# Weight passes three steps later, early high stores, first MoE products after the products with v, and MoE operands at multiples of 512 bytes

## The chip, the cores and the metric

The kernel runs on one core of a Trainium2 chip. The number that counts is the device time of one execution in microseconds (us). Before the change the median of three runs is 692.88 us (692.36 to 696.8).

## What is computed

An attention layer with a learned position bias, and behind it an MLP with a rational activation. Shapes: 4 batches, 8 heads, 576 positions, head width 64; then 2304 tokens of width 512 and a hidden width of 2048.

```python
scores = scale * np.matmul(q, k.transpose(0, 1, 3, 2)) + bias   # bias: 8 heads x 576 x 576, from a small MLP
attn = np.exp(scores - scores.max(-1))                          # divided by its sum + 1e-9
x = (attn @ v).transpose(0, 2, 1, 3).reshape(2304, 512)
h = x @ w_in
P = a[0] + a[1] * h + a[2] * h**2 + a[3] * h**3
Q = 1.0 + abs(b[0]) * abs(h) + abs(b[1]) * h**2
out = (P / (Q + 1e-6)) @ w_out
```

All inputs are float32, except that `w_in` and `w_out` arrive as float64.

## The kernel before

**Attention** is 72 steps, `step_a(i)`. In a step TensorE (PE) makes the scores of one block of queries for a pair of heads (`sc`, L324, float32), transposes the weights `p` of two steps ago (`tp` and a small piece in `mx`, L393), and multiplies the transposed weights `pt` of three steps ago with `v` (into `mx`, L433). VectorE (DVE) adds the bias and takes the row maximum `m` (L334); ScalarE (ACT) makes the exponential (L350) and a copy of `tp` (L401); DVE copies the rest of it and the result `xs` (L412, L443). GpSimd (POOL) multiplies `xs` with the reciprocal sums (`e_norm`, L382), one per pair of heads and batch; these go through DRAM (`xd`) and come back as the MoE input `xr`.

**Weight passes.** The MoE multiplies in a reduced float32 kind, with every operand split into a high and a low part. While the attention runs, the float64 weights are turned into such pairs, piece by piece: 16 pieces (`f`) for each of the two matrices. A piece is loaded as `wx` and `wy` (SP queue, L120, L121) and goes through `mag` (DVE, L130, makes `wk`), `rebias` (ACT, L135, makes `wh`), `sign` and `join` (DVE, L138, L144), `low` (POOL, or DVE for the last six of `f`, L156, makes `wil`, `wol` or `wl`) and `store` (SP queue, L160 into `wih` or `woh`, or to DRAM as `ws`, L107 and L108). `wk` has one buffer; `wh`, `wl`, `wx` and `wy` have two, so that the third piece's `rebias` waits for the first one's store to land. `in_order` lays all these out in one list, and `run_jobs`, at the end of every attention step, works it off up to and with one DVE pass.

**MoE** is 48 steps over 12 groups of 384 tokens, with the weights in four groups: groups 0 to 2 stand in tiles `wih0` to `wol2`, the fourth is cut out of a bias tile that has become free (`wg`). Each step has 24 matmuls `h <- x * w_in` (`mm1`, L300, 384 columns; the moving operand is `xh` or `xl`, the stationary one `wih` or `wil`) and, for the step two before, 18 matmuls `o <- g * w_out` (L766, 512 columns; moving `woh` or `wol`, stationary `gh` or `gl`). Between the two stands the activation on ACT, POOL and DVE: `w`, `u`, `t`, `r`, then `gh` (DVE, L714), `m` (L721, L728) and `gl` (POOL, L735). The tokens of an even group are held in tiles of pool `xp`, those of an odd group in `xp2`. The remaining weight passes (the late six) run beside the first 25 or so MoE steps on DVE.

Where a tile begins in a partition of SBUF is set by the order and size of the tiles allocated before it, from the left end for some pools and from the right end for others. In the built program the offsets in a partition, taken modulo 512 bytes, are 448 for `wih`, `wil`, `woh`, `wol` of groups 0 to 2 and for `xh`, `xl` of even groups; they are 64 for `wg`, for `xh`, `xl` of odd groups, and for `gh`, `gl`.

Of the kernel before, what the change touches and what calls it, by code (L numbers as in the profile page):

```python
# [16 lines left out]
P = 128  # L17
# [16 lines left out]
def tile_attn_moe(  # L34
# [49 lines left out]

    stg = ctx.enter_context(tc.tile_pool(name="stg", bufs=2))
# [19 lines left out]
    def w_out_to(f, part, hi, lo):  # L105
        d = dpool.tile([P, 2, KD, P], F32, tag=f"ws{f}_{part}", name=f"ws{f}_{part}")
        nc.sync.dma_start(out=d[:, 0], in_=hi.bitcast(F32))  # L107
        nc.sync.dma_start(out=d[:, 1], in_=lo.bitcast(F32))  # L108
        wsc[f, part] = d

    def w_conv(f, part):
# [21 lines left out]

        def rebias():
            A.activation(out=tl("wh", U32, 2), in_=st["wk"], func=AF.Relu, bias=wmin, scale=8.0)  # L135

        def sign():
            V.scalar_tensor_tensor(  # L138
                out=st["wh"], in0=st["u"], scalar=0x80000000, in1=st["wh"],
                op0=ALU.bitwise_and, op1=ALU.bitwise_or,  # L140
            )

        def join():
            V.scalar_tensor_tensor(  # L144
                out=tl("wk", U32), in0=st["m"], scalar=13, in1=st["wh"],
                op0=ALU.logical_shift_right, op1=ALU.bitwise_or,
            )

        def low():
            x, hi = st["wk"].bitcast(F32), st["wh"].bitcast(F32)  # L150
            if here:
                out = w_hilo(f, part)[1]
                x, hi = (v.rearrange("p (k f) -> p k f", k=KD) for v in (x, hi))
            else:
                out = tl("wl", F32R, 2)
            eng.tensor_tensor(out=out, in0=x, in1=hi, op=ALU.subtract)  # L156

        def store():
            if here:
                nc.sync.dma_start(  # L160
                    out=w_hilo(f, part)[0].bitcast(F32),
                    in_=st["wh"].bitcast(F32).rearrange("p (k f) -> p k f", k=KD),
                )
                return
            w_out_to(
                f, part, st["wh"].rearrange("p (k f) -> p k f", k=KD),
                st["wl"].rearrange("p (k f) -> p k f", k=KD),
            )
# [3 lines left out]
    def w_plain(f, part):  # L172
        st = {}

        def load():
            st["x"] = stg.tile([P, KD, P], F32, tag="wx", name=f"wx{f}_{part}")
            nc.sync.dma_start(out=st["x"], in_=w_src(f, part))

        def hi():
            st["h"] = stg.tile([P, KD, P], F32R, tag="wh", name=f"wh{f}_{part}")  # L180
            A.copy(out=st["h"], in_=st["x"])

        def lo():
            st["l"] = stg.tile([P, KD, P], F32R, tag="wl", name=f"wl{f}_{part}")
            V.tensor_tensor(out=st["l"], in0=st["x"], in1=st["h"].bitcast(F32), op=ALU.subtract)

        return [load, [], [hi], [lo, lambda: None, lambda: w_out_to(f, part, st["h"], st["l"])]]
# [4 lines left out]
    def in_order(jobs, after):  # L192
        seq = [("sp", j[0]) for j in jobs[:2]]
        end = []
        for i, (_, first, act, last) in enumerate(jobs):
# [3 lines left out]
            seq += [("dve", x) for x in ops[1:]] + [("low", low)]  # L199
            if i + 2 < len(jobs):  # L200
                seq.append(("sp", jobs[i + 2][0]))
            end = [("sp", x) for x in [store] + after.get(i, [])]
# [15 lines left out]
    with tc.manual_schedule():  # L218
# [3 lines left out]
        with ExitStack() as actx:  # L222
# [266 lines left out]
            def step_a(i):  # L489
# [25 lines left out]
                if i == NS + 1:  # L515
                    mm1(0, 1)
                if ok(TL + 1):
                    pv = e_pv(i - TL - 1, mx)
                if ok(0):
# [7 lines left out]
                if i == NS - 1:  # L527
                    mm1(0, 0)
# [22 lines left out]
                if i >= 2:  # L551
                    run_jobs(i >= 5 and (c > 0 or g % 2 == 0))
# [116 lines left out]
            G.memset(wpool.tile([P, 8], F32, tag="edge", name="edge"), 0.0)  # L669
# [266 lines left out]
```

## Time and profile before

| | us |
|---|---|
| median of three runs | 692.88 |
| the profiled execution | 693.02 |
| its span (first to last instruction) | 691.2 |
| PE busy | 671.3 (97%) |
| DVE busy | 578.1 (84%) |
| ACT busy | 484.8 (70%) |
| POOL busy | 233.8 (34%) |

The profiled execution lies 1.8 us outside its span, and 0.1 us above the median. Matmuls overlap, so a busy PE is not a PE at its peak: how fast it runs is read from the distance between the starts of like matmuls. The page also follows the chain of work that ended last back from the end and gives each engine's share of it. In a timeline row, the bracket at the end says how long the engine stood idle before the row and whose end released it.

### The profile page before, as it was taken

Reading aid. Unit: us, or ns where it says so; the run is one execution under the profiler, and the core shown is the slowest. Engines: PE = TensorE matmul, PEld = TensorE weight load, DVE = VectorE, ACT = ScalarE, POOL = GpSimd, SP = SyncE. Lnnn points to the kernel's source line nnn. Section 1 sums busy time; section 2 is a strip of 40 time slices with the busy share of each in tenths; the row PEclk is TensorE's granted clock in tenths of the full one; section 3 lists DMA queues with packets and bytes.
Section 4 is the critical chain, followed back from the end, with each engine's and each line's share of the span. In section 5 each row is a group of like instructions: output and inputs, shape, how many; then the busy total and the mean of one; then the engine's idle time right before and its main releaser. Section 6 shows DMA issues by size and latency. Waiting matters only on the chain.

```text
span 691.2 us, 16655 instructions
## 1 busy us (share of the span) xinstructions
PE 671.3 (97%) x6450; PEld 577.8 (84%) x6450; DVE 578.1 (84%) x1032; ACT 484.8 (70%) x758; POOL 233.8 (34%) x144
## 2 busy tenths in 40 slices
PE   6999899999999999999999999999999999999997
PEld 3777688888878778888999999999999999999995
DVE  7995788888878787499999999999968787878666
ACT  5888688889898888576666757676755565655561
POOL 0010032212312221164444544444444445344442
PEclk9999999999999999999999999999999999999999
DMA  4887998988898997324444443579621212122021
GB/s 139 310 310 222 352 306 267 319 260 272 295 342 278 299 334 252 98 105 157 160 169 143 134 177 135 169 226 297 231 91 47 92 46 92 46 91 93 1 92 46
DMA packets 77583, 129.50 MB, mean 187 GB/s; under 512 B 12208, under 2 KB 33856, under 8 KB 77504
## 3 DMA queue, kind: packets, MB, share of 16 engines
q1 hardware_dynamic: 76640, 126.77, 54.7%
q10 hardware_dynamic: 864, 1.67, 0.8%
q8 instruction: 51, 0.84, 0.5%
q14 instruction: 28, 0.23, 0.1%
HBM read 89.65 MB, written 35.61 MB: 181 GB/s over the span
## 4 chain that ended last, share of the span: by engine, by line
PE 85%; DVE 5%; DMA 4%; issue 2%; ACT 2%; SPq 1%; POOL 0%; DVEq 0%; ACTq 0%; POOLq 0%
PE o L766 27%; PE h L300 27%; PE mx L433 11%; PE sc L324 10%; PE tp L393 5%; PE pb L635 5%; DMA wih<-wh 2%; DVE ring L597 1%; DVE gh L714 1%; DMA ws<-wh 1%; PE mx L393 1%; DMA wy<-in_w_in_dram 1%; ACT pt L401 1%; DMA cst<-in_cst_dram 1%; DMA tab<-e 1%
## 5 line engine op out<-in xcount | busy, mean ns | idle before, releaser
L696 POOL TENSOR_TENSOR u<-u,w 128x768 f32<-128x768 f32 x48 | 96.7, 2015 | 159.1 <-ACT u L694 155.5
L334 DVE CUSTOM_DVE_ANT_0 s<-sc,bias 128x576 f32<-128x576 f32 x144 | 103.6, 754 | 18.7 <-PE sc L324 11.5
L350 ACT ACTIVATE p<-s,m 128x576 f32<-128x576 f32 x144 | 110.7, 772 | 1.5 <-DVE m L334 1.1
L693 ACT ACTIVATE w<-h 128x768 f32<-128x768 f32 x48 | 39.0, 813 | 102.1 <-PE h L300 102.1
L735 POOL TENSOR_TENSOR gl<-m,r 128x768 fp32r<-128x768 f32 x47 | 87.2, 1855 | 57.0 <-DVE m L728 54.9
L300 PE MATMUL h<-xl,wih 128*128 128x384 f32 x288 | 97.0, 337 | 0.3 <-DVE xl L286 0.3
L300 PE MATMUL h<-xh,wih 128*128 128x384 f32 x288 | 97.3, 338 | 0.0
L300 PE MATMUL h<-xh,wil 128*128 128x384 f32 x288 | 97.0, 337 | 0.0
L324 PE MATMUL sc<-k,q 64*128 64x288 f32 (+1 forms) x640 | 92.6, 428 | 4.0 <-DVE m L334 4.0
L433 PE MATMUL mx<-pt,v 128*64 128x128 f32 (+1 forms) x1600 | 95.6, 268 | 0.9 <-DVE xs L443 0.9
L401 ACT COPY pt<-tp 128x1024 f32<-128x1024 f32 x72 | 72.3, 1005 | 20.5 <-PE tp L393 20.3
L766 PE MATMUL o<-woh,gh 128*128 128x512 f32 x216 | 85.2, 395 | 0.0
L766 PE MATMUL o<-wol,gh 128*128 128x512 f32 x216 | 85.1, 394 | 0.0
L433 PEld LDWEIGHTS mx<-pt,v 128*64 128x64 f32 x1600 | 79.1, 137 | 6.1 <-ACT u L694 1.1
L700 ACT ACTIVATE r<-u,qc 128x768 f32<-128x768 f32 x48 | 45.1, 940 | 36.8 <-POOL u L696 36.3
L324 PEld LDWEIGHTS sc<-k,q 64*128 64x128 f32 (+1 forms) x640 | 50.3, 175 | 24.4 <-DVE m L334 9.1
L704 DVE TENSOR_TENSOR t<-t,h 128x768 f32<-128x768 f32 x48 | 45.5, 949 | 30.0 <-ACT t L695 24.5
L721 DVE SCALAR_TENSOR_TENSOR m<-u,qc,gh 128x768 f32<-128x768 f32 x48 | 61.8, 1288 | 5.4 <-DVE gh L714 0.5
L728 DVE SCALAR_TENSOR_TENSOR m<-t,cst,m 128x768 f32<-128x768 f32 x48 | 64.2, 1337 | 1.7
L714 DVE SCALAR_TENSOR_TENSOR gh<-t,cst,r 128x768 fp32r<-128x768 f32 x48 | 56.5, 1176 | 8.2 <-ACT r L701 5.8
L766 PE MATMUL o<-woh,gl 128*128 128x512 f32 x216 | 56.2, 395 | 0.0
L300 PEld LDWEIGHTS h<-xl,wih 128*128 128x128 f32 x288 | 54.1, 188 | 2.1 <-DVE xl L286 0.7
(73 smaller groups left out, 1284.3 us busy)
## 6 DMA issues: line engine op xcount, KB each, us to landing
tab<-e SPq DMA_DIRECT2D x36, 295.5 KB, 4.3
wx<-in_w_in_dram SPq DMA_DIRECT2D x16, 512.0 KB, 5.5
wy<-in_w_in_dram SPq DMA_DIRECT2D x16, 512.0 KB, 6.3
wx<-in_w_out_dram SPq DMA_DIRECT2D x16, 512.0 KB, 4.5
wy<-in_w_out_dram SPq DMA_DIRECT2D x16, 512.0 KB, 5.9
xr<-xd SPq DMA_DIRECT2D x7, 768.0 KB, 6.8
ws<-wh SPq DMA_DIRECT2D x20, 256.0 KB, 2.0
ws<-wl SPq DMA_DIRECT2D x20, 256.0 KB, 2.9
```

Of the source, the lines that this page charges most:

```text
L300: T.matmul(hps[s][:, j, :TT], w[:, k, sl], x[:, k, :], start=(k == 0 and z == 0), stop=(k == KD - 1 and z == 2),)
L324: T.matmul(sc[i, j][o, a, :SH], q[r, x], k[r, a * SH:(a + 1) * SH], start=True, stop=True,)
L334: V.tensor_tensor_reduce(out=t.rearrange("p (a s) -> p a s", a=2), in0=sc.pop((i, j))[:, :, :SH], in1=bias[p][:, 5 * j + c, :].rearrange(" ...
L350: A.activation(out=prob[i][:, z * S:z * S + S], in_=t, func=AF.Exp, bias=m, scale=-1.0, accum_out=sums[u % 4][:, k:k + 1],)
L401: A.copy(out=t[:, 0:8].rearrange("p x (r s) -> p r x s", r=2), in_=ps)
L433: T.matmul(ps[y, o], vt[n][:, kc, y], t[:, 2 * kc + j if kc < 4 else 8, o], start=(kc == 0), stop=(kc == 4),)
L696: G.tensor_tensor(out=u, in0=u, in1=w, op=ALU.mult)
L714: V.scalar_tensor_tensor(out=hi, in0=rt[s, "t"], scalar=abs_[:, 0:1], in1=rt[s, "r0"], op0=ALU.add, op1=ALU.mult,)
L721: V.scalar_tensor_tensor(out=m, in0=rt[s, "u"], scalar=qc, in1=rt[s, "gh"].bitcast(F32), op0=ALU.add, op1=ALU.mult,)
L728: V.scalar_tensor_tensor(out=m, in0=rt[s, "t"], scalar=abs_[:, 0:1], in1=m, op0=ALU.add, op1=ALU.subtract)
L735: eng.tensor_tensor(out=lo, in0=rt[s, "m"], in1=rt[s, "r0"], op=ALU.mult)
L766: T.matmul(po[n, c], l[:, j, c * P:(c + 1) * P], r[fp][:, j, :], start=(first and x is a), stop=(last and x is z),)
```

## The change

Four things change; no operation of DVE or ACT gets another shape.

1. **Where tiles begin.** A tile of 448 bytes per partition (`fill`, with one small memset on POOL) is put ahead of the pools on the left, and the tile `edge` on the right grows from 32 to 480 bytes. In the built program `wih`, `wil`, `woh`, `wol`, `wg`, `xh`, `xl`, `gh`, `gl` and the activation's tiles now all begin at offset 0 modulo 512. Of the attention's tiles, `p` goes from 448 to 384 while the constant `ident` stays at 128; `q` and `k`, and `pt` and `v`, move together.
2. **The store in two.** The high part's store is issued right after `join`, ahead of `low` and of the next piece's loads; the low part's store (to DRAM only) stays where the whole store was.
3. **When passes run.** The DVE passes begin at step 8 instead of 5, loads at step 4 instead of 2, and no step is left out any more (before, steps 11, 29, 47 and 65 had none). So a pass stands three steps later until step 11, two until 29, one until 47, at its old step until 65, and one step earlier behind that.
4. **The first MoE products.** `mm1(0, 0)` moves from the end of step 71 to step 72 behind its products with `v`, and `mm1(0, 1)` in step 73 from before them to behind them.

```diff
+    fill = cpool.tile([P, 112], F32, tag="fill", name="fill")
+    nc.gpsimd.memset(fill[:, 0:8], 0.0)
...
-            seq += [("dve", x) for x in ops[1:]] + [("low", low)]
+            seq += [("dve", x) for x in ops[1:]] + [("sp", lambda st=store: st(True, False)), ("low", low)]
             if i + 2 < len(jobs):
                 seq.append(("sp", jobs[i + 2][0]))
-            end = [("sp", x) for x in [store] + after.get(i, [])]
+            end = [("sp", x) for x in [lambda st=store: st(False, True)] + after.get(i, [])]
...
-                if i == NS + 1:
-                    mm1(0, 1)
                 if ok(TL + 1):
                     pv = e_pv(i - TL - 1, mx)
+                if 0 <= i - NS < 2:
+                    mm1(0, i - NS)
...
-                if i == NS - 1:
-                    mm1(0, 0)
...
-                if i >= 2:
-                    run_jobs(i >= 5 and (c > 0 or g % 2 == 0))
+                if i >= 4:
+                    run_jobs(i >= 8)
...
-            G.memset(wpool.tile([P, 8], F32, tag="edge", name="edge"), 0.0)
+            G.memset(wpool.tile([P, 120], F32, tag="edge", name="edge"), 0.0)
```

`store(hi, lo)` issues for a piece that stays in SBUF the one copy of the high part, and for the others the high or the low part's copy to DRAM.

On PE at the change from attention to MoE, before (`h0` and `h1` are the products `mm1` of the first two MoE steps, one row standing for twelve or more; `mx72` to `mx74` and `tp70`, `tp71` belong to steps 72 to 74):

```order
L300 MATMUL h0_5168<-xh0_4512,wih0_934 128x384
...
L393 MATMUL mx72_5189<-ident_60,p70_5114 128x64 x2
L393 MATMUL tp70_5191<-ident_60,p70_5114 128x64 x16
L433 MATMUL mx72_5189<-pt69_5129,v15_4586 64x128 x10
L393 MATMUL mx73_5225<-ident_60,p71_5166 128x64 x2
L393 MATMUL tp71_5227<-ident_60,p71_5166 128x64 x16
...
L300 MATMUL h0_5168<-xl0_4513,wih0_934 128x384
L300 MATMUL h0_5168<-xh0_4512,wil0_935 128x384
L433 MATMUL mx73_5225<-pt70_5190,v15_4586 64x128 x10
L433 MATMUL mx74_5279<-pt71_5226,v15_4586 64x128 x10
L300 MATMUL h1_5298<-xh0_4512,wih1_938 128x384
```

The same place after:

```order
L391 MATMUL mx72_5178<-ident_60,p70_5116 128x64 x2
L391 MATMUL tp70_5180<-ident_60,p70_5116 128x64 x16
L431 MATMUL mx72_5178<-pt69_5131,v15_4590 64x128 x10
L298 MATMUL h0_5210<-xh0_4514,wih0_936 128x384
...
L391 MATMUL mx73_5227<-ident_60,p71_5168 128x64 x2
L391 MATMUL tp71_5229<-ident_60,p71_5168 128x64 x16
...
L431 MATMUL mx73_5227<-pt70_5179,v15_4590 64x128 x10
L298 MATMUL h0_5210<-xl0_4515,wih0_936 128x384
L298 MATMUL h0_5210<-xh0_4514,wil0_937 128x384
L431 MATMUL mx74_5281<-pt71_5228,v15_4590 64x128 x10
L298 MATMUL h1_5300<-xh0_4514,wih1_940 128x384
```

Twelve `h0` matmuls now stand between the products of `pt69` and the transposes of `p71`, and the other twelve between the products of `pt70` and those of `pt71`, which were back to back.

On the SP queue near the start of the weight passes, before (`q2` to `v2` are operands of the third pair of heads):

```order
L120 DMA wx0_0_990<-in_w_in_dram 128x1024
L121 DMA wy0_0_991<-in_w_in_dram 128x2048
L120 DMA wx0_1_994<-in_w_out_dram 128x1024
L121 DMA wy0_1_995<-in_w_out_dram 128x2048
L253 DMA q2_1048<-in_qt_dram 128x576
L254 DMA k2_1049<-in_kt_dram 128x576
L260 DMA v2_1152<-in_vp_dram 128x640
```

After:

```order
L251 DMA q2_1042<-in_qt_dram 128x576
L252 DMA k2_1043<-in_kt_dram 128x576
L123 DMA wx0_0_1095<-in_w_in_dram 128x1024
L124 DMA wy0_0_1096<-in_w_in_dram 128x2048
L123 DMA wx0_1_1099<-in_w_out_dram 128x1024
L124 DMA wy0_1_1100<-in_w_out_dram 128x2048
L258 DMA v2_1152<-in_vp_dram 128x640
```

The four loads of the first two pieces are now behind `q2` and `k2`; their first use on DVE is three steps later. Further on, a high store stands ahead of the next loads on this queue, where it stood behind them.

## Rows read from the trace of the kernel before

**Rows 1.** The page: each engine's share of the chain that ended last.
```profile
PE 85%; DVE 5%; DMA 4%; issue 2%; ACT 2%; SPq 1%; POOL 0%; DVEq 0%; ACTq 0%; POOLq 0%
```
**Rows 2.** Windows: stretch, us, busy PE, PEld, DVE, ACT, POOL, PEclk, DMA share, GB/s.
```profile
60.00:80.00 20.00, 17.06 (x240) 13.49 (x238) 11.38 (x36) 13.06 (x27) 0.71 (x1) 0.91 0.88 306
240.00:260.00 20.00, 18.80 (x308) 15.70 (x308) 17.09 (x53) 17.47 (x36) 4.14 (x3) 1.00 0.97 319
```
**Rows 3.** Timeline of PE, scores of steps 5 to 8: start, us, instruction, idle before.
```profile
63.73 1.24 PE L324 MATMUL sc<-k,q 64*128 64x288 f32 x8
66.70 1.20 PE L324 MATMUL sc<-k,q 64*64 64x288 f32 x16
72.79 2.09 PE L324 MATMUL sc<-k,q 64*128 64x288 f32 x7 [2.94 <-DVE m L334]
77.99 1.24 PE L324 MATMUL sc<-k,q 64*128 64x288 f32 x8
```
**Rows 4.** Timeline of the SP queue and of DVE: the first piece's load and pass.
```profile
66.85 0.43 SPq L120 DMA_DIRECT2D wx<-in_w_in_dram  x1
71.63 0.43 DVE L130 TENSOR_SCALAR wk<-wx 128x512 uint32<-128x512 uint32 x1 [4.32 <-DMA wx<-in_w_in_dram]
```
**Rows 5.** Timeline of ACT: two passes that waited for a store.
```profile
190.78 0.72 ACT L135 ACTIVATE wh<-wk,wmin 128x512 uint32<-128x512 uint32 x1 [2.39 <-DMA wih<-wh]
231.68 0.72 ACT L135 ACTIVATE wh<-wk,wmin 128x512 uint32<-128x512 uint32 x1 [2.31 <-DMA ws<-wh]
```
**Rows 6.** Timeline of PE: the scores around those two passes.
```profile
189.97 1.24 PE L324 MATMUL sc<-k,q 64*128 64x288 f32 x8
194.33 1.24 PE L324 MATMUL sc<-k,q 64*128 64x288 f32 x8
230.88 1.20 PE L324 MATMUL sc<-k,q 64*64 64x288 f32 x16
235.23 1.24 PE L324 MATMUL sc<-k,q 64*128 64x288 f32 x8
```
**Rows 7.** Timeline of PE where the MoE begins.
```profile
281.03 0.28 PE L393 MATMUL mx<-ident,p 64*128 64x64 f32 x2 [0.68 <-DVE xs L443]
286.27 1.31 PE L433 MATMUL mx<-pt,v 128*64 128x128 f32 x20 [0.87 <-DVE xs L443]
```
**Rows 8.** Timeline of PE: first and last of four stretches of like matmuls.
```profile
411.01 0.33 PE L300 MATMUL h<-xh,wih 128*128 128x384 f32 x1
...
414.48 0.34 PE L300 MATMUL h<-xh,wil 128*128 128x384 f32 x1
...
414.65 0.39 PE L766 MATMUL o<-woh,gh 128*128 128x512 f32 x1
...
417.20 0.40 PE L766 MATMUL o<-wol,gh 128*128 128x512 f32 x1
...
424.40 0.39 PE L766 MATMUL o<-wg,gh 128*128 128x512 f32 x1
...
426.89 0.40 PE L766 MATMUL o<-wg,gl 128*128 128x512 f32 x1
...
444.08 0.34 PE L300 MATMUL h<-xl,wih 128*128 128x384 f32 x1
...
447.95 0.34 PE L300 MATMUL h<-xh,wil 128*128 128x384 f32 x1
```
**Rows 9.** Windows, columns as in rows 2: four MoE steps with weight passes.
```profile
326.70:360.20 33.50, 33.50 (x170) 30.36 (x169) 32.67 (x34) 21.54 (x29) 15.72 (x8) 1.00 0.46 153
```
**Rows 10.** Timeline of POOL: `gl` of MoE steps 3 and 23.
```profile
321.04 1.84 POOL L735 TENSOR_TENSOR gl<-m,r 128x768 fp32r<-128x768 f32 x1 [3.17 <-DVE m L728]
...
485.92 1.87 POOL L735 TENSOR_TENSOR gl<-m,r 128x768 fp32r<-128x768 f32 x1
```
**Rows 11.** Timeline of DVE: the same operation twice.
```profile
300.01 2.61 DVE L714 SCALAR_TENSOR_TENSOR gh<-t,cst,r 128x768 fp32r<-128x768 f32 x1
...
497.71 1.00 DVE L714 SCALAR_TENSOR_TENSOR gh<-t,cst,r 128x768 fp32r<-128x768 f32 x1
```

More of the change, by code (lines that the diff above doesn't have):

```diff
@@ L105, in w_out_to @@
     def w_out_to(f, part, hi, lo):
-        d = dpool.tile([P, 2, KD, P], F32, tag=f"ws{f}_{part}", name=f"ws{f}_{part}")
-        nc.sync.dma_start(out=d[:, 0], in_=hi.bitcast(F32))
-        nc.sync.dma_start(out=d[:, 1], in_=lo.bitcast(F32))
+        d = wsc.get((f, part)) or dpool.tile([P, 2, KD, P], F32, tag=f"ws{f}_{part}", name=f"ws{f}_{part}")
         wsc[f, part] = d
+        for i, t in enumerate((hi, lo)):
+            if t is not None:
+                nc.sync.dma_start(out=d[:, i], in_=t.bitcast(F32))
     def w_conv(f, part):
@@ L132, in mag, with rows @@
             )
+        def rows(t):
+            return t.rearrange("p (k f) -> p k f", k=KD)
         def rebias():
-            A.activation(out=tl("wh", U32, 2), in_=st["wk"], func=AF.Relu, bias=wmin, scale=8.0)
+            st["wh"] = rows(tl("wh", U32, 2))
+            A.activation(out=st["wh"], in_=rows(st["wk"]), func=AF.Relu, bias=wmin, scale=8.0)
         def sign():
             V.scalar_tensor_tensor(
-                out=st["wh"], in0=st["u"], scalar=0x80000000, in1=st["wh"],
+                out=st["wh"], in0=rows(st["u"]), scalar=0x80000000, in1=st["wh"],
                 op0=ALU.bitwise_and, op1=ALU.bitwise_or,
@@ L144, in join @@
             V.scalar_tensor_tensor(
-                out=tl("wk", U32), in0=st["m"], scalar=13, in1=st["wh"],
+                out=rows(tl("wk", U32)), in0=rows(st["m"]), scalar=13, in1=st["wh"],
                 op0=ALU.logical_shift_right, op1=ALU.bitwise_or,
@@ L149, in low, with store @@
         def low():
[L150 to L167, printed above, removed]
-            )
+            st["wl"] = w_hilo(f, part)[1] if here else rows(tl("wl", F32R, 2))
+            eng.tensor_tensor(
+                out=st["wl"], in0=rows(st["wk"]).bitcast(F32), in1=st["wh"].bitcast(F32), op=ALU.subtract
+            )
+        def store(hi=True, lo=True):
+            if not here:
+                w_out_to(f, part, st["wh"] if hi else None, st["wl"] if lo else None)
+            elif hi:
+                nc.sync.dma_start(out=w_hilo(f, part)[0].bitcast(F32), in_=st["wh"].bitcast(F32))
         return [load, [mag], [rebias], [sign, join, low, store]]
@@ L185, in lo @@
             V.tensor_tensor(out=st["l"], in0=st["x"], in1=st["h"].bitcast(F32), op=ALU.subtract)
-        return [load, [], [hi], [lo, lambda: None, lambda: w_out_to(f, part, st["h"], st["l"])]]
+        return [load, [], [hi], [lo, lambda: None, lambda hi=True, lo=True: w_out_to(f, part, st["h"] if hi else None, st["l"] if lo else None)]]
     def w_job(f, part):
```

## Prediction

> **What bounds the kernel now.** First the page's share of the chain that ended last: PE has 85% of it, no other engine more than 5% [rows 1]. So the question in each stage is how fast PE runs there and what interrupts it. Second the timeline of PE in the attention, at the starts of the scores: an undisturbed step is 66.70 − 63.73 = 2.97 us [rows 3]; longer steps are losses, and the bracket on a waiting instruction says to whom. Third the timeline of PE in the MoE, where it never waits: there the spacing of like matmuls counts [rows 8]. Last the windows, to see who would be next: DVE is busy 32.67 of 33.50 us in four MoE steps with weight passes [rows 9], and DMA 97% of the time late in the attention [rows 2].
>
> **Attention: first passes.** From the scores of step 6 to those of step 8 PE needs 77.99 − 66.70 = 11.29 us instead of 2 × 2.97 = 5.94: a loss of 5.35 [rows 3]. The first DVE pass (L130) stands there 4.32 us for its load `wx`, issued at 66.85 and ready at 71.63 [rows 4]; behind it on DVE are the row maxima on which the scores wait 2.94 us [rows 3]. The rest is the clock: after that idle time PE is granted 0.91 of it over 60 to 80 us, against 1.00 later [rows 2]. The changed order has this pass three steps later. DVE reached it at 71.63 − 4.32 = 67.31, so now at 67.31 + 3 × 2.97 = 76.2. Its load is behind `q2` and `k2`, 128 × 576 × 4 bytes = 0.295 MB each; at the 306 GB/s of that window [rows 2] they cost 1.9 us, so `wx` is there at about 71.6 + 1.9 = 73.5. That leaves 2.7 us of cover; were it gone, the loss would return as it was. Nothing else on DVE waits for `wx`, and the matmuls of steps 6 and 7 do not need the pass. I take 5.35 as won.
>
> **Attention: stores.** The third piece's `rebias` on ACT needs a `wh` buffer, free when the first piece's store has landed. Two such waits are long, 2.39 and 2.31 us [rows 5], and there the steps take 194.33 − 189.97 = 4.36 and 235.23 − 230.88 = 4.35 us, 1.39 and 1.38 over 2.97 [rows 6]. Issuing the high store right after `join`, a step (2.97) earlier, covers both. But the SP queue now holds this store ahead of the loads, and the DMA engines are 97% busy late in the attention [rows 2]: the same bytes have to move, and a wait on a store can come back as a wait on a load. Bounds: all 2.77, or a new wait as long, −2.77. I take a quarter, 0.65, since the total traffic is unchanged. What is queued behind the store on SP (`q`, `k`, `v` and bias loads) waits only if `join` is late; a pass is issued in the step that computes it, so I cost that at nothing (covered by operand loads that are issued steps ahead). Attention together: **6.0**, between 5.35 − 2.77 = 2.6 and 8.1.
>
> **The entry to the MoE.** Before, PE waits 0.68 us for `xs` ahead of a product's tile and 0.87 ahead of a product with `v` [rows 7], while matmuls of `mm1(0, ·)` that need neither have already been spent. Moved behind the products they stand in those gaps: twelve matmuls of some 0.17 us (below) are 2.1 us each time, more than either wait. Sum 0.68 + 0.87 = 1.55; I take **1.6** with its bounds 0 (the chain of copies on DVE sets the start anyway) and 2.0. Their end is needed by the first activation, which starts as much earlier as PE does.
>
> **MoE: the matmul spacing.** This is the largest new thing. In an even group (step 16) `xh` and `wih` are both at 448 modulo 512: 20 intervals from 411.01 to 414.48 are 173.5 ns each. In an odd group (step 20) they are at 64 and 448: 22 intervals from 444.08 to 447.95 are 175.9 ns. In the second product, `woh` at 448 against `gh` at 64: 11 intervals from 414.65 to 417.20, 231.8 ns; `wg` and `gh` both at 64: 11 from 424.40 to 426.89, 226.4 ns [rows 8]. So it is the equality of the two offsets, not a place, that goes with the short spacing: 448 with 448 and 64 with 64 both have it. After the change all pairs are equal (0 and 0). Per step: 24 × 173.5 + 18 × 226.4 ns = 8.24 us. Before: the last `h` matmuls four steps apart stand at 414.48 and 447.95, 33.47 / 4 = 8.37 us [rows 8]. By kinds (half of the first products unequal, three quarters of the second) the same rows give 24 × 174.7 + 18 × 230.5 = 8.34, so 0.03 of the 0.13 may lie between the stretches and stay. Gain 0.10 to 0.13 per step; I take 0.12.
>
> **Who would be next there.** DVE is 97% busy in those steps [rows 9]. From the end of `gl` in step 3 (321.04 + 1.84 = 322.88) to its end in step 23 (485.92 + 1.87 = 487.79) are 164.91 us, 8.25 per step [rows 10]; this chain has been a little faster than PE's 8.37 and is about what PE would now need, 8.24. It permits just the gain forecast and no more while passes run. Over the first three or four steps DVE and POOL set the pace (`gl` waits 3.17 us for DVE [rows 10]), so no gain there. The other 44 steps: 44 × 0.12 = **5.3**. Bounds: 20 steps with nothing and the rest at 0.10 gives 2.4; 48 × 0.13 gives 6.2.
>
> A row on this pair of engines: the same `gh` takes 2.61 us at one place and 1.00 at another [rows 11], the longer beside POOL work. [...]
>
> **Small items.** `fill`'s memset and the larger `edge` run on POOL, which has 4.14 of 20 us of work even late in the attention [rows 2]: nothing. `ident` and `p` change their offsets against each other (320 to 256); equal and unequal pairs in float32 here show no such difference that I can price, so ±1 us goes into the range. POOL's `e_norm` ahead of `low`: by the same row POOL has the time: nothing.
>
> **The sum.** 693.0 − 6.0 − 1.6 − 5.3 = 680.1 for the profiled execution, 0.1 less against the median: **680.0 us**.
>
> **The rivals.**
> (A) As above, 676 to 684 with the terms' bounds taken half together: 0.62.
> (B) The offsets do not set the spacing; something that goes with even groups and with `wg` does (another pool, another bank, what is loaded meanwhile). For: only four combinations of offsets stand in the trace, none of them 0. Against: two independent products agree. Then 693.0 − 6.0 − 1.6 − 0.1 = 685.3. Chance 0.12.
> (C) The attention gives back what it wins: loads later and stores earlier meet in the 97% busy DMA engines, and only 2 us of the 6.0 stay: 684. Against: the loads' total is the same, and the first-pass loss has 2.7 us of cover. Chance 0.13. That the early store alone does nothing falls under this.
> (D) Offset 0 is better than merely equal, so that the spacing falls below 173.5 and 226.4. Nothing in the rows shows it; were it worth what equality is worth in the second product, 231.8 − 226.4 = 5.4 ns [rows 8], for all 42 matmuls of a step, that is 0.23 us a step in the 24 steps without passes (in the others DVE's 8.25 holds it): 5.4 us, about 674.6. Chance 0.07. [...]
> (E) Slower: with PE's pace now equal to that of DVE's chain, the phase between them slips so that in each of 23 steps one more DVE operation falls onto POOL's. Each costs 2.61 − 1.00 = 1.61 us [rows 11], and DVE, with 0.83 us of idle in four steps [rows 9], has no room: 23 × 1.61 = 37 us, at 680.1 + 37 + 2.3 (the lost gain of those steps) about 719. The kernel is no faster from (693.0 − 682.4) / 23 = 0.46 us a step, two more collisions in seven steps. For: one such collision stands in most steps already. Against: DVE's order does not change, and the same chain stayed in phase over 20 steps. Chance 0.06, of which 0.04 beyond 1%.
>
> **How the numbers follow.** One per cent, 6.9 us, is about what a measurement of this kernel can tell from no change; faster then means below 686.0. Faster: 0.60 from A, 0.07 from B (which lies close to the bound), 0.08 from C, 0.07 from D and none from E: 0.82. Slower: 0.04. The same: the remaining 0.14. The range of 673.5 to 687 leaves out E, the low end of D and the far ends of the others, about 2 in 10.
>
> **What would show each step.** In the trace after: `wk` of the first piece without a wait, the scores of steps 6 to 8 at 2.97 us and PE's clock at 1.00 in 60 to 80 us; no wait on `wih<-wh` or `ws<-wh` over 1 us at ACT's L135; no wait of PE for `xs` where the MoE begins; first products at 173 ns in even and odd groups alike, second products at 226 for all weights; and 8.24 to 8.27 us per MoE step. The prediction is wrong if the spacing of the first product in odd groups stays at 176 ns, if a stall like that of step 7 appears at another pass, or if DVE's steps to step 23 become longer than 8.25 us.

## The result and the profile after

The changed kernel takes 687.42 us (median of four runs, 681.12 to 688.26) against 694.13 us for the kernel before (median of four, the three of the table above among them): a ratio of 0.990, 95% interval 0.9862 to 0.9938. Two later measurements on other chips gave 0.9914 (0.9883 to 0.9946) and 0.9934 (0.9909 to 0.996). It is faster, by about 0.9% and not by the 1.9% forecast, and 687.42 lies just outside the range of 673.5 to 687. The profiled execution took 688.26 us, the slowest of the four, so what single stretches show below is one execution's. Its page (span, PE's busy time, shares of the chain that ended last):

```profile
span 686.5 us, 16650 instructions
PE 669.5 (98%) x6450; PEld 577.8 (84%) x6450; DVE 580.7 (85%) x1032; ACT 485.6 (71%) x758; POOL 235.7 (34%) x145
PE 78%; DMA 5%; DVE 5%; issue 2%; ACT 1%; POOL 1%; SPq 0%; DVEq 0%; POOLq 0%; ACTq 0%
```

The span is 4.7 us shorter. Where they come from, worked out in the two traces from the first row maximum (DVE) of attention steps 5, 11, 40 and 71 and from the starts of the second products (PE) of MoE steps 0, 4, 24 and 44:

| stretch | before | after | won | forecast |
|---|---|---|---|---|
| before attention step 5 | 65.10 | 64.64 | 0.46 | 0 |
| steps 5 to 11 | 23.37 | 18.16 | 5.21 | 5.35 |
| steps 11 to 40 | 87.75 | 87.42 | 0.33 | 0.65 |
| steps 40 to 71 | 98.24 | 102.73 | −4.49 | with the line above |
| step 71 to the first second product | 21.51 | 20.59 | 0.92 | 1.6 |
| MoE steps 0 to 4 | 34.97 | 36.12 | −1.15 | 0 |
| MoE steps 4 to 24 | 167.36 | 166.04 | 1.32 | 2.4 |
| MoE steps 24 to 44 | 171.72 | 170.29 | 1.43 | 2.4 |
| rest | 21.18 | 20.51 | 0.67 | 0.5 |

The last interval of steps 24 to 44 holds two stretches of first products (12.55 us before, 12.47 after); the other MoE steps from step 4 on take 8.37 us on average before and 8.30 after.

**The first passes** went as foreseen. On the timeline (SP queue, DVE, PE) the load is issued a little later and is there when DVE comes to it three steps later, with no wait in the bracket [rows 4]; the scores of steps 6 to 9 stand 3 us apart [rows 3]; and the window of 60 to 80 us has PE at the full clock [rows 2]:

```profile
67.50 0.44 SPq L123 DMA_DIRECT2D wx<-in_w_in_dram  x1
...
76.06 0.40 DVE L133 TENSOR_SCALAR wk<-wx 128x512 uint32<-128x512 uint32 x1
```
```profile
66.25 1.20 PE L322 MATMUL sc<-k,q 64*64 64x288 f32 x16
69.33 1.24 PE L322 MATMUL sc<-k,q 64*128 64x288 f32 x8
72.30 1.24 PE L322 MATMUL sc<-k,q 64*128 64x288 f32 x8
75.34 1.24 PE L322 MATMUL sc<-k,q 64*128 64x288 f32 x8
```
```profile
60.00:80.00 20.00, 20.00 (x340) 16.44 (x338) 14.13 (x47) 17.44 (x36) 0.00 (x0) 1.00 0.89 305
```

What this is worth varies with the execution: steps 5 to 11 take 18.1 to 18.2 us in every trace with the late start, and 20.35 (e1), 22.85 (e6) and 24.16 us (e3) in the other traces with the old pass times, beside the 23.37 above.

**The stores.** The waits of `rebias` on a store [rows 5] are gone. In their place the timeline has, late in the attention, `mag` waiting for a load and PE behind it. ACT waits for the MoE's input, with PE behind that, for 3.54 us; this wait is not new, it took 2.16 us (at 244.75) in the kernel before:

```profile
215.84 0.43 DVE L133 TENSOR_SCALAR wk<-wx 128x512 uint32<-128x512 uint32 x1 [2.58 <-DMA wx<-in_w_out_dram]
214.39 1.31 PE L431 MATMUL mx<-pt,v 128*64 128x128 f32 x20
217.00 1.67 PE L322 MATMUL sc<-k,q 64*128 64x288 f32 x7 [1.30 <-DVE m L332]
219.77 2.40 PE L431 MATMUL mx<-pt,v 128*64 128x128 f32 x20
241.76 0.51 ACT L283 CAST xh<-xr 128x384 fp32r<-128x384 f32 x1 [3.54 <-DMA xr<-xd]
243.10 0.28 PE L391 MATMUL mx<-ident,p 64*128 64x64 f32 x2 [1.29 <-ACT p L348]
```

With the wait at 217.00 more than its 1.30 us is lost. Behind it PE's clock is granted at one half from 219.0 to 222.4 us (PEclk 0.50 in that window), and the products with `v` take 2.40 us there instead of 1.31. The kernel before has a fall of the same length at 73.9 us (0.50 to 77.3), behind the wait of the first pass; it is part of what the late start wins. At half the clock 3.4 us hold 1.7 us less work (an estimate from these figures), so this much came back late. Windows of the kernel before and of the changed one (columns as in rows 2):

```profile
220.00:240.00 20.00, 18.94 (x310) 15.46 (x306) 16.09 (x48) 16.51 (x34) 3.97 (x3) 1.00 0.93 300
```
```profile
220.00:240.00 20.00, 20.00 (x311) 16.50 (x311) 15.07 (x47) 15.39 (x30) 3.97 (x3) 0.94 0.93 299
```

The traces of e2, e4 and e15 below have such a fall at 244 us, those of e5, e13, e14, e17 and e18 have none in the attention from step 5 on.

How the load came to be late is read on the SP queue: `join` ends at 201.16 + 0.68 = 201.84 us, but the store behind it is issued only 8.3 us later, and the load after the store:

```profile
201.16 0.68 DVE L151 SCALAR_TENSOR_TENSOR wk<-wy,wh 128x512 uint32<-128x512 uint32 x1
...
210.14 0.84 SPq L112 DMA_DIRECT2D ws<-wh  x1
211.02 0.43 SPq L123 DMA_DIRECT2D wx<-in_w_out_dram  x1
```

So the store was not issued "right after join": the queue was 8 us behind. Over the first 18 pieces the high store is issued 4.9 us after `join` on average, where the whole store of the kernel before came after 6.3, and the load `wx` of the second piece on 5.7 us after `join`, where it came after 2.5. The store gained 1.4 us, and the load behind it lost 3.2.

**The entry to the MoE.** PE no longer waits for `xs` there [rows 7]. But on ACT's timeline the first activation starts at 284.25 us in the kernel before and at 284.00 in the changed one:

```profile
284.25 0.81 ACT L693 ACTIVATE w<-h 128x768 f32<-128x768 f32 x1 [1.33 <-PE h L300]
```
```profile
284.00 0.81 ACT L689 ACTIVATE w<-h 128x768 f32<-128x768 f32 x1 [2.56 <-PE h L298]
```

The attention's last step began 1.5 us earlier, so measured from there the activation is 1.3 us later: the second half of `h0` now stands behind the products of `pt70`.

**The MoE's spacing.** A stretch of first products and the stretch before it of second ones, both with equal offsets (timeline of PE):

```profile
412.69 0.39 PE L762 MATMUL o<-woh,gh 128*128 128x512 f32 x1
...
414.77 0.39 PE L762 MATMUL o<-wol,gh 128*128 128x512 f32 x1
...
416.81 0.33 PE L298 MATMUL h<-xh,wih 128*128 128x384 f32 x1
...
417.88 0.33 PE L298 MATMUL h<-xh,wih 128*128 128x384 f32 x1
...
420.82 0.33 PE L298 MATMUL h<-xh,wil 128*128 128x384 f32 x1
421.00 0.39 PE L762 MATMUL o<-wg,gh 128*128 128x512 f32 x1
```

From the seventh first product on the spacing is (421.00 − 417.88) / 18 = 173.3 ns, as forecast [rows 8]; but the first six take 1.07 / 6 = 178 ns. Of the second products the first nine take 2.08 / 9 = 231 ns, and the other nine (416.81 − 414.77) / 9 = 226.7. So it is in the 37 such steps between 330 and 640 us: 177.6 and 173.3 ns, 230.9 and 226.7 on average. A step takes 8.30 us and not 8.24.

### The profile page after: what moved, and what is told of

Read it like the earlier page. It is cut to its first block, busy times and chain, and to the rows that moved or that the text cites. A ratio compares the mean times of both kernels' runs of the same rounds, so it can differ in the third digit from the quotient of the medians.

```text
span 686.5 us, 16650 instructions
## 1 busy us (share of the span) xinstructions
PE 669.5 (98%) x6450; PEld 577.8 (84%) x6450; DVE 580.7 (85%) x1032; ACT 485.6 (71%) x758; POOL 235.7 (34%) x145
## 2 busy tenths in 40 slices
DMA packets 77583, 129.49 MB, mean 189 GB/s; under 512 B 12209, under 2 KB 33857, under 8 KB 77505
## 4 chain that ended last, share of the span: by engine, by line
PE 78%; DMA 5%; DVE 5%; issue 2%; ACT 1%; POOL 1%; SPq 0%; DVEq 0%; POOLq 0%; ACTq 0%
PE o L762 27%; PE h L298 26%; PE mx L431 10%; PE sc L322 10%; PE tp L391 4%; DMA bias<-tab 1%; DMA wy<-in_w_out_dram 1%; DVE gh L710 1%; PE mx L391 1%; DMA xr<-xd 1%; DMA rb<-rs 1%; DMA wx<-in_w_in_dram 1%; DMA wx<-in_w_out_dram 1%; DVE s L332 1%; DVE xl L284 1%
## 5 line engine op out<-in xcount | busy, mean ns | idle before, releaser
L692 POOL TENSOR_TENSOR u<-u,w 128x768 f32<-128x768 f32 x48 | 97.6, 2034 | 126.1 <-ACT u L690 108.3
L710 DVE SCALAR_TENSOR_TENSOR gh<-t,cst,r 128x768 fp32r<-128x768 f32 x48 | 66.1, 1377 | 7.7 <-ACT r L697 5.3
L717 DVE SCALAR_TENSOR_TENSOR m<-u,qc,gh 128x768 f32<-128x768 f32 x48 | 58.7, 1223 | 5.0
L724 DVE SCALAR_TENSOR_TENSOR m<-t,cst,m 128x768 f32<-128x768 f32 x48 | 57.9, 1207 | 1.7
```

Source lines behind the costliest of these rows:

```text
L692: G.tensor_tensor(out=u, in0=u, in1=w, op=ALU.mult)
L710: V.scalar_tensor_tensor(out=hi, in0=rt[s, "t"], scalar=abs_[:, 0:1], in1=rt[s, "r0"], op0=ALU.add, op1=ALU.mult,)
L717: V.scalar_tensor_tensor(out=m, in0=rt[s, "u"], scalar=qc, in1=rt[s, "gh"].bitcast(F32), op0=ALU.add, op1=ALU.mult,)
L724: V.scalar_tensor_tensor(out=m, in0=rt[s, "t"], scalar=abs_[:, 0:1], in1=m, op0=ALU.add, op1=ALU.subtract)
```

## The experiments

All times are medians; "before" is the kernel before, measured beside the run on the same chip. The ratio is that of the executions, not the quotient of the two medians. The stretches that are named stand in the one profiled execution of each run.

| run | us | before | ratio, 95% interval |
|---|---|---|---|
| e1 offsets alone | 690.59 | 692.36 | 0.997 (0.9944 to 0.9996) |
| e2 schedule alone | 692.41 | 692.36 | 0.9988 (0.9958 to 1.0017) |
| e3 all at 64 | 690.65 | 692.36 | 0.9987 (0.9952 to 1.0022) |
| e4 changed kernel | 687.72 | 693.98 | 0.9914 (0.9883 to 0.9946) |
| e5 whole store | 684.17 | 693.98 | 0.9875 (0.9838 to 0.9912) |
| e6 old pass times | 691.75 | 693.98 | 0.9977 (0.9953 to 1.0002) |
| e7 no low stores | 687.03 | 693.98 | 0.9896 (0.9866 to 0.9926) |
| e8 whole store, old first products | 685.03 | 693.42 | 0.9878 (0.9836 to 0.9919) |
| e9 load ahead of store | 687.92 | 693.42 | 0.9903 (0.9873 to 0.9934) |
| e10 whole store, steps left out | 685.99 | 693.42 | 0.9877 (0.984 to 0.9914) |
| e11 whole store | 686.77 | 693.18 | 0.991 (0.9878 to 0.9942) |
| e12 stores in halves | 702.68 | 693.18 | 1.0112 (1.0077 to 1.0146) |
| e13 e11 with few `rb` loads | 680.51 | 693.18 | 0.9821 (0.9794 to 0.9849) |
| e14 changed, few `rb` loads | 680.22 | 693.18 | 0.9816 (0.9787 to 0.9845) |
| e15 changed kernel | 690.24 | 693.81 | 0.9934 (0.9909 to 0.996) |
| e16 changed, tiny `rb` loads | 687.17 | 693.81 | 0.9913 (0.9884 to 0.9942) |
| e17 whole store, `rb` in pairs | 681.98 | 693.81 | 0.984 (0.9806 to 0.9874) |
| e18 changed, `rb` in pairs | 685.17 | 693.81 | 0.987 (0.9831 to 0.9909) |

### The two halves of the change, and what an offset is worth

e1 puts `fill` and the larger `edge` into the kernel before; e2 takes them out of the changed one. e3 leaves `fill` out and moves the right side alone:

```diff
-            G.memset(wpool.tile([P, 8], F32, tag="edge", name="edge"), 0.0)
+            G.memset(wpool.tile([P, 104], F32, tag="edge", name="edge"), 0.0)
```

> Only the offsets change (fill and the larger edge on the kernel before); passes, stores and first products stand as before. Theory S (the MoE gain was real but over-sized, because the first 6 to 9 matmuls of every stretch stay slow whatever the offsets): a MoE step takes 8.30 us instead of 8.37, all 44 steady steps give about 3.1 us, the attention is unchanged, and the time is 3 to 4 us below the kernel before. Rival (the offsets also speed up the attention's transfers): 5 us or more below it, with a lower DMA share in the attention. Rival (offsets do nothing, the difference in the MoE came with the schedule): no change, 8.37 us a step.

> The changed kernel without fill and with the small edge: offsets as before, but passes, stores and first products moved. Theory S with theory T (the attention gives most of its gain back to the loaded DMA engines): first passes without the wait for wx, 2 to 5 us gained in all, later waits on wx between 180 and 260 us as in the changed kernel, 8.37 us a MoE step. Rival (the moved schedule and the offsets only work together): no gain at all.

> The kernel before with edge at 104 columns and no fill: all MoE operands begin at 64 modulo 512, so they are equal but not at a multiple of 512. If equality sets the spacing: 8.30 us a MoE step, as in e1, and the same time as e1 within 1 us. If the multiple of 512 sets it: 8.37 us, and the time of the kernel before.

In the traces, MoE steps 24 to 44 take 170.30 us in e1, 170.29 in e3 and 171.72 in e2, against 171.72 before and 170.29 in the changed kernel; steps 4 to 24 take 166.26, 166.09 and 167.36. In these runs equal offsets are what counts, and 64 is as good as 0. In 320 to 650 us of e3 (groups of instructions: count, busy, mean ns) and of the kernel before:

```profile
L766 PE MATMUL o<-wol,gh 128*128 128x512 f32 x180 | 70.6, 392 | 0.0
L766 PE MATMUL o<-woh,gl 128*128 128x512 f32 x176 | 44.8, 389 | 0.0
```
```profile
L766 PE MATMUL o<-wol,gh 128*128 128x512 f32 x176 | 69.3, 394 | 0.0
L766 PE MATMUL o<-woh,gl 128*128 128x512 f32 x174 | 45.2, 395 | 0.0
```

`gl`, which is the last third of each stretch, gains most; that is the part behind the slow beginning. The MoE gives 3 us with either of the equal offsets, whatever the attention does. The whole times of e1 to e3 scatter by as much: the attention from step 5 to step 71 is 207.36, 207.57 and 209.74 us there. Together e1 and e2 lie 2.9 us under the kernel before in ratio, the whole change 4.6 to 6.9; the intervals do not settle whether there is more to the two together. e2 shows less than the 2 to 5 us that I expected, and its time alone does not exclude its rival; in its trace the late start is won (steps 5 to 11 take 18.1 us) and lost again behind step 40 (101.6 us against 98.2).

### Is it a fixed place, the store, the pass times?

e4 and e15 repeat the changed kernel. e5 and e11 undo the store:

```diff
-            seq += [... ("sp", lambda st=store: st(True, False)), ("low", low)]
+            seq += [... ("low", low)]
...
-            end = [("sp", x) for x in [lambda st=store: st(False, True)] + after.get(i, [])]
+            end = [("sp", x) for x in [store] + after.get(i, [])]
```

e6 has the old `run_jobs` lines in the changed kernel; e8 is e5 with the two `mm1` calls back at their old places; e9 puts the high store, in the same step, behind the next load instead of ahead of it; e10 is e5 with `run_jobs(i >= 8 and (c > 0 or g % 2 == 0))`.

> The changed kernel once more, to have a second trace and more times beside the variants of this call. Theory T (the waits on loads late in the attention come from DMA engines that are full, so they fall on other passes in each execution): again 5 to 9 us below the kernel before, executions several us apart, with late loads at other steps than in the first trace. Rival (a fixed place in the order, such as a store ahead of a load): the same steps 44, 53 and 65 are long again.

> The changed kernel with the store whole and at its old place, a step later and behind the next loads. Theory O (the high store ahead of the next loads makes these late): the waits of mag on wx go, 3 us or more faster than the changed kernel. Theory T: same time within 2 us, since the bytes are the same; waits of rebias on the store come back at some steps (2 us each).

> The changed kernel with the passes at their old steps (from step 5, with the steps left out as before), the loads from step 2. Theory T: the wait of the first pass on wx is back (5 us), but the loads later on have more room and the waits there go, so about the time of the changed kernel, at most 2 us slower. Rival (the gain of the late start stays): 4 to 6 us slower than the changed kernel.

> As e5 (whole store at its old place), and the first MoE products back at their old places. Theory M (the move earns the two waits of PE for xs, but starts the first activation later against the attention's end, so that the first four MoE steps lose it again): the entry is 0.9 us longer, the first four steps 1.2 us shorter, and the time that of e5 within 1 us, rather 0.3 us below it. Rival (the move is worth the 1.6 us of the prediction): 1 to 2 us slower than e5.

> The changed kernel with the high store still in the step of its join, but behind the next piece's loads on the queue instead of ahead of them. Theory O (the harm is that the loads stand behind the store): as e5 or better, 2 to 4 us faster than the changed kernel, no long wait of mag on wx, and the waits of rebias on the store shorter than in e5. Rival (the split itself, or a store closer to the join, is what costs): as the changed kernel.

> As e5, but with a step without a pass again at the four places where there was one before (the passes then end a few steps later). Theory P (packing passes closer costs late in the attention, since transfers have less time): 1 to 3 us faster than e5. Rival (it is only the late start and the order of store and load that count): as e5 within 1 us.

> The kernel of e5 once more, on the chip of the next three, as their base. Expected 684 to 686 us, 1.1 to 1.3% below the kernel before, and DMA engines at 0.96 to 0.98 over 66 to 160 us, moving 311 to 315 GB/s there.

e4: the long steps are 53 and 56 (a load) and 61 and 62 (the MoE's input); step 44 is not among them, 53 is again. So neither purely fixed nor purely by chance.

e6: the old times cost 4.0 us on the same chip, with the step-5 wait back (6.62 us for that step), so the late start does stay won. The rival was right there, and my expectation of "at most 2" wrong.

e5 is 3.5 us faster than e4. Its load is issued 2.6 us after `join` (200.30 + 0.68 = 200.98), where the changed kernel needs 9.2 for the same load:

```profile
200.30 0.68 DVE L151 SCALAR_TENSOR_TENSOR wk<-wy,wh 128x512 uint32<-128x512 uint32 x1
```
```profile
203.61 0.52 SPq L123 DMA_DIRECT2D wx<-in_w_out_dram  x1
```

But e9, with the load ahead of the store, is no faster than the changed kernel, and its loads are mostly issued 3 to 8 us after `join` all the same: theory O falls. e11, the kernel of e5 on another chip, is at 0.991, inside the intervals of the changed kernel. By the times the place of the store costs 2 to 3 us at best estimate: four ratios with the store early (the result, e4, e9, e15) are 0.990 to 0.9934, four with the store whole (e5, e8, e10, e11) are 0.9875 to 0.991. The traces say the same without an overlap. Steps 11 to 71 take 189.3 to 190.2 us with the early store (the changed kernel, e2, e4, e6, e9, e15) and 184.1 to 188.6 with the whole one (e5, e8, e10, e11), where the old schedule has 185.6 to 187.0 (the kernel before, e1, e3). No run shows a gain of the early store. Why e9 costs as much, with the store behind the load, is not shown.

e8: the entry is 21.53 us with the old places and 20.60 with the new ones, MoE steps 0 to 4 take 34.87 and 36.16: the move wins 0.93 and loses 1.29. e10: as e5 within the intervals, so theory P is not borne out.

### Bytes, packets or instructions

e7 leaves out the low stores to DRAM. e12 splits each store of e11 into two DMA instructions; e13 and e14 leave out two small loads per pair of heads and batch; e16 keeps these as instructions of one packet. In e13, e14 and e16 alike POOL's multiplication is an eighth narrower.

```diff
 e12
-                nc.sync.dma_start(out=d[:, i], in_=t.bitcast(F32))
+                for k in (0, 2):
+                    nc.sync.dma_start(out=d[:, i, k:k + 2], in_=t[:, k:k + 2].bitcast(F32))
...
 e13, e14 (the whole instruction left out), e16 (one packet)
-                        out=o[:, 512:S],
-                        in_=rl[8 + j:9 + j, z:z + 64].to_broadcast([64, 64]),
+                        out=o[0:1, 512:S],
+                        in_=rl[8 + j:9 + j, z:z + 64],
...
```

> The changed kernel without the stores of the low parts to DRAM (20 of 256 KB, those from the seventh piece on; the later loads read the high part twice, so the computation is changed there). It takes 5.2 MB of traffic out of the second half of the attention and the start of the MoE and nothing else. Theory T: the late loads after 190 us go, the attention's steps there return to 2.97 us, and the time falls by 3 to 5 us below the changed kernel. Rival (the waits come from the order of the queue or from DVE): no change beyond 1 us.

> As e11, but each store goes as two DMA instructions of half the size: the same bytes at the same place of the queue, in twice the instructions. In the built program each DMA of the SP queue waits for the one eight places ahead of it. Theory W (those eight places are what holds the DMA engines below their best when large transfers stand together or small ones take the places): the DMA engines move less over 66 to 160 us (under 310 GB/s), and it is 1 to 3 us slower than e11. Rival (only the place of the store against join and loads counts): as e11 within 1 us.

> As e11, without the two 16 KB loads of rb per pair of heads and batch (the last 64 positions are not divided by their sums, and POOL's multiplication is an eighth narrower): 32 DMA instructions less with 0.5 MB in all. Theory W: the SP queue has two more places of eight free around each wx load, 1 to 2 us faster than e11. Rival (the bytes bind): same as e11 within 1 us, since 0.5 of 60 MB is nothing.

> The changed kernel with the same two loads of rb left out (the last 64 positions are not divided by their sums). Theory W: gets back 2 us or more of what the early store costs, 685 us or less, with wx issued earlier after join and fewer waits of mag on wx. Rival (only the place of the store counts): as the changed kernel, 687 us, within 1 us.

> The changed kernel a third time, on the chip of the next three, as their base. Expected 686 to 689 us, with executions 5 us apart.

> The changed kernel with the two small loads of rb kept as instructions, but each of one packet of 256 bytes instead of 64 (as in e14 the last 64 positions are not divided by their sums). The number of DMA instructions is that of the changed kernel, the packets are nearly those of e14. If e14 was fast because 32 places of the eight were free (theory W): as the base, 686 to 688 us. If it was fast because 2,500 small packets take the DMA engines several us (theory K): as e14, 680 to 682 us.

e7 is inconclusive: its profiled execution is its fastest (683.36 us, with short steps late in the attention), but the median of seven is that of the changed kernel.

e12 is 16 us slower than e11 with the same bytes, where I expected 1 to 3. It has more packets too (84,303 against 77,583), but its DMA engines are less busy (0.89 against 0.95 in e11), so they are not what holds it up. Some 5 of the 16 us are the clock, which stands at one half for 13.7 us in the attention against 3.4 in e11 (an estimate, half of the difference; the granted clock is 0.93 and 0.94 over 160 to 210 and 210 to 266 us of e12, 1.00 and 0.97 in e11). e13 and e14 are 6 and 7 us faster than e11 and the changed kernel, though only 0.5 MB is gone, and the executions of each lie within 3.4 us of each other. e16, which has the packets of e14 but the instructions of the changed kernel, is at 687.17, close to its base (690.24, intervals overlapping) and 7 us above e14. So it is the number of DMA instructions on the queue; to the packets the two medians leave some 3 us.

The windows of 66 to 266 us (columns as in rows 2) of the kernel before, the changed kernel, e12 and e14 show more bytes moved where fewer instructions stand on the queue (310 GB/s in e14, 281 to 304 in the others), with the DMA engines less than full in all four, 0.89 to 0.93:

```profile
66.00:266.00 200.00, 193.57 (x3132) 159.06 (x3128) 162.57 (x490) 171.36 (x340) 41.36 (x31) 0.99 0.92 300
```
```profile
66.00:266.00 200.00, 195.09 (x3141) 161.08 (x3139) 162.80 (x498) 172.67 (x343) 43.17 (x32) 0.99 0.93 304
```
```profile
66.00:266.00 200.00, 187.53 (x2938) 153.05 (x2934) 151.95 (x459) 158.73 (x315) 39.99 (x30) 0.97 0.89 281
```
```profile
66.00:266.00 200.00, 200.00 (x3299) 166.48 (x3296) 168.85 (x515) 179.28 (x355) 43.00 (x33) 1.00 0.93 310
```

In e14 PE is busy in all of the 200 us. The SP queue in the same 200 us, added up from its timeline and its waits:

| kernel | DMA instructions | issuing, us | waiting for an earlier DMA to land | waiting for an engine |
|---|---|---|---|---|
| before | 253 | 133.8 | 42.0 | 22.0 |
| changed | 256 | 132.6 | 51.5 | 16.1 |
| e11 | 256 | 132.2 | 48.8 | 14.5 |
| e12 | 256 | 141.6 | 43.0 | 14.9 |
| e14 | 235 | 119.9 | 37.8 | 40.9 |
| e17 | 250 | 126.1 | 42.9 | 28.8 |

Issuing and waiting for landings fill 176 to 185 of 200 us in the first four kernels of the table, and about 255 instructions get through, even when each store is half as big (e12): 0.78 us apiece. The sum alone does not order the runs: it is 166 us in e1 (steps 5 to 71 in 207.4 us) and 181 in e8 (203.6 us). In the built program each DMA on this queue waits until the one eight places ahead has landed; in the trace of the changed kernel 458 of 468 use the semaphore of the one eight places ahead. Whether it is that or the 0.5 us of issuing that counts more, these runs do not separate. In e14 the queue has 41 us left in which it waits for its producers: it no longer sets the pace. There the early store is issued 0.4 us after `join` on average, as the prediction wanted it, and the load behind it after 1.2; and e13 and e14, whole store and early store, take the same time (680.51 and 680.22 us).

### A faster kernel

e17 loads the small parts of `rb` once for two pairs of heads, on top of e5; e18 does the same in the changed kernel.

```diff
...
-                    nc.sync.dma_start(
-                        out=o[:, 512:S],
-                        in_=rl[8 + j:9 + j, z:z + 64].to_broadcast([64, 64]),
-                    )
+                    if u % 2 == 0:
+                        nc.sync.dma_start(
+                            out=rbt[0][64 * j:64 * j + 64],
+                            in_=r[8 + j:9 + j, :].to_broadcast([64, P]),
+                        )
...
-                eng.tensor_tensor(out=x, in0=x, in1=rb.pop(u), op=ALU.mult)
+                eng.tensor_tensor(out=x[:, 0:512], in0=x[:, 0:512], in1=rb.pop(u)[:, 0:512], op=ALU.mult)
+                eng.tensor_tensor(out=x[:, 512:S], in0=x[:, 512:S], in1=rbt[0][:, z:z + 64], op=ALU.mult)
```

> A complete kernel: the whole store at its old place, and the small parts of rb loaded once for two pairs of heads (512-byte packets into a tile of their own, 16 instructions and 1,000 packets instead of 32 and 2,000), for which POOL's multiplication is two instructions. Theory W and theory K both give it half of the gain of e13 over e11, 682 to 684 us. If POOL's extra instructions cost more than that, 686 us or more.

> The same on the changed kernel, with its early high store: again about half of the gain of e14, 683 to 685 us, by theories W and K both. If it is as fast as e17, the place of the store no longer counts once the queue has room.

e17 takes 681.98 us, 1.6% below the kernel before (its interval lies below that of the changed kernel on the same chip, 0.9909 to 0.996), and in its trace PE is busy without a gap over the 200 us, with 312 GB/s moved:

```profile
66.00:266.00 200.00, 200.00 (x3308) 166.84 (x3308) 168.59 (x518) 179.67 (x355) 47.41 (x46) 1.00 0.94 312
```

Half of e13's gain over e11 (6.3 us) was expected. By the ratios it is 0.7% or 4.9 us ahead of e11 and 0.35% or 2.4 us ahead of e5, the same kernel without the pairs on other chips, so the half is about met and not settled closer. e18 lies at 685.17; whether the store's place still costs the 3 us between them stays open, as their intervals overlap.

## Why the prediction failed, step by step

Of the 12.9 us forecast (6.0, 1.6 and 5.3) the two spans show 4.7. By the table the stores fell short by 4.8 us, the entry with the first four MoE steps by 1.8 and the spacing by 1.9; the first passes are right within 0.2.

**First passes, right.** 5.35 us were forecast, 5.21 won, at the place named and with the mechanism named (wait gone, clock at 1.00, 3 us between the scores); e6 shows that it takes the late start. That the two figures are so close is partly luck, as the loss with the old pass times is 2.2 to 6.0 us from trace to trace.

**Stores, wrong, and this is the step that failed.** The prediction took 0.65 us of gain for the split and costed it at nothing on the SP side: "a pass is issued in the step that computes it". In the changed kernel the store is issued 0.2 to 9.3 us after its `join`, 4.9 on average over 18 pieces: 1.4 us earlier than before and not a step of 2.97, while the loads behind it come 3.2 us later. Steps 11 to 71 took 4.2 us more than before instead of 0.65 less, an estimated 1.7 of it in the fall of the clock behind the wait at 217.00. A stall like that of step 7 at another pass was one of the prediction's own signs of being wrong, and it is there. The prediction read 97% busy DMA engines [rows 2] as a bound by bytes and expected at worst one new wait of 2.77 us; but 0.97 is the share of one window, and over 66 to 266 us it is 0.92. The bound is the queue ahead of the engines, some 255 DMA instructions in 200 us (e12, e13, e14, e16). On the full queue the early store gave back what the late start had won: with the same list of instructions and the store whole, e5, e8 and e10 keep it (202.3 to 203.6 us from step 5 to step 71, against 209.4 before and 208.3 in the changed kernel; e11, at 206.8, keeps less). Rival C (the attention gives back what it wins, 684 us, chance 0.13) named the outcome, with the DMA engines instead of the queue as its cause. With fewer instructions on the queue the attention gives the forecast and more even with the early store: e14 is at 680.22 us, with 199.7 us from step 5 to step 71, though e14 leaves out a part of the work. How much of the 4.2 us is the store's place in every execution stays open; the times say 2 to 3 us.

**The entry, wrong in its second half.** The waits of PE were covered as said, 0.92 us instead of 1.6. But "the first activation, which starts as much earlier as PE does" was false, since the end of `h0` was moved behind `pt70`, and the first four steps took 36.12 us instead of 34.97, with 1.2 us of waits of PE for `gl` (POOL) between 276 and 322 us, where the kernel before has none. Net −0.2 us, just below the lower bound given (0).

**The MoE's spacing, right mechanism, wrong size.** Equality of offsets sets the spacing (MoE steps 24 to 44 take 170.30 us in e1 and 170.29 in e3, against 171.72 before; rival B falls), and 0 is no better than 64 (rival D falls). The offsets of the MoE operands in these runs are equal or 384 bytes apart; other distances were not tried. No run shows the low end of D that the forecast's range leaves out: with offset 0 the settled spacings are 173.3 and 226.7 ns, beside 173.5 and 226.4 for equal offsets before. The term was 0.12 us a step and measured 0.07, because both the rows [rows 8] and the sum went by the settled part of each stretch. The first six to nine matmuls after each change of product keep their slow spacing, with equal offsets too (177.6 and 230.9 ns in the changed kernel). The 0.03 us that the prediction could not place was a first sign of it.

**Who is next, not reached.** DVE's 8.25 us per step [rows 10] never bound, as PE stayed at 8.30. Rival E did not come: steps 4 to 24 became shorter, not longer (166.04 us against 167.36).

## What to carry to other kernels

Before moving a transfer in a busy queue, compare when it is issued with when its data is ready: here the store was issued 4.9 us after `join`, and its earlier place won 1.4 us for it and lost 3.2 for the load behind it. Count the queue's instructions in a busy stretch and add up issuing and waiting for landings. Here these filled 176 to 185 of 200 us; leaving out 32 loads of 16 KB, 0.5 MB in all, was worth 6 to 7 us, merging them in pairs 2.4 to 4.9 (e17), and the place of the store 2 to 3. When a wait is removed in one place, look whether the clock falls behind another, as it did here at 219.0 us, to 0.50 for 3.4 us. A spacing measured in the settled part of a stretch must be checked against the length of the whole stretch before it is multiplied: 0.12 us a step was forecast here and 0.07 measured.

## What was not expected of the hardware

The SP queue handled 253 to 256 DMA instructions in 200 us in the kernel before, the changed one, e11 and e12 (247 to 257 in the other runs with the full list of small loads), with stores whole or halved, and the DMA engines moved 281 to 306 GB/s accordingly. A wait of PE of 1.3 us was followed by 3.4 us at half the clock (0.50 from 219.0 us of the changed kernel), and one of 1.29 us at 243.10 in the same trace by none (1.00 over 243 to 252 us). After the switches between the two products from 330 to 640 us of the changed kernel, PE's spacing is 178 ns on average over six matmuls of 384 columns and 231 ns over nine of 512, then 173.3 and 226.7, even with equal offsets; what sets this beginning was not tried.
